# The first unit's attention transfers go through a paced queue, v loads follow the visit, and one pair of activations moves

## The chip, the cores and the metric

The kernel runs on one core of one Trainium2 chip. A core has a matrix engine (TensorE, PE in the profile, with its weight loads as PEld), a vector engine (VectorE, DVE), an activation engine (ScalarE, ACT), a general engine (GpSimd, POOL) and a fifth instruction queue without arithmetic (SyncE, SP), which in this kernel issues most DMA transfers. Each engine works through its own list of instructions in order and waits on semaphores for the others. The metric is the device time of one execution in microseconds, the median of several runs.

## The reference

Two computations follow each other. First comes attention with normalized q and k, over 8 batches, 12 heads, 448 positions and a head size of 64, in float32:

```python
def rmsnorm(x, g):
    rms = np.sqrt(np.mean(x * x, axis=-1, keepdims=True) + 1e-06)
    return x / rms * g
q_n, k_n = (rmsnorm(q, g_q), rmsnorm(k, g_k))
scores = scale * np.matmul(q_n, k_n.transpose(0, 1, 3, 2))
attn = np.exp(scores - np.max(scores, axis=-1, keepdims=True))
attn = attn / (np.sum(attn, axis=-1, keepdims=True) + 1e-09)
return np.matmul(attn, v)
```

Its result, laid out as 3584 tokens by 768 features, goes through a feed-forward layer with 2048 hidden features:

```python
h = np.maximum(x @ w_in, 0.0)
return (h * h @ w_out)
```

## The kernel before, in words

**Units and pairs.** Heads are taken two at a time, so that 64 + 64 features fill the 128 partitions: 48 pairs, six to a batch. The feed-forward layer takes two batches at a time; this is a *unit*, four in all. The matrix products of the feed-forward layer are done in Strassen-like forms (seven products in place of eight), in the later units two levels deep.

**What runs beside what.** The first twelve pairs have nothing beside them (`visit_alone`). From then on the attention of the next two batches is woven into the feed-forward layer of the two before. `ffn(u)` is a generator: each `yield` hands out one step of matrix products, with its cost. `run(until)` takes steps until a cost is reached; after each step it may convert a piece of weights, make sums of weights, and take the next pieces of attention work from the queues `tasks` and `pool_tasks`. Between two calls of `run` stands a *visit* of a pair, which puts down scores, exponentials and the product with v of the neighbouring pair. The *first unit* is the stretch in which `first` is true while `ffn(0)` runs, here some 137 to 530 us of the span: one level of Strassen (`first_products` at L909, `second_products` at L1077 and L1138), in four blocks of some 96 us.

**What the first unit does besides.** It also reads the weights. Each piece of 384 KB comes as 32-bit words into one of three buffers (`load_weights`, L1232 and L1237). ACT splits it (`split_words`, L1251 to L1253), DVE joins it (L1264, L1284, L1288), and the buffer is free for the piece after the next two. Then the sums that the products need are made (L1364), and the forms for the later units are stored in DRAM: five large stores for each block (`raw`, L1314 and L1316), ten sums made on DVE (L1324) in four buffers named `more`, each stored at L1342, and finished `out_sb` tiles at L1366.

**Attention's transfers.** For a pair of the later batches, q and k are loaded (`load_qk`, normalized on POOL at L217), q is stored to DRAM (`store_q`, name `q_rows`), and both are read back in 32-column blocks, two halves for each head (`load_blocks`), so that DVE can transpose them block by block (`turn_blocks`, L351). A load of q's blocks waits for the store. v comes with `load_v` (L361, and L368 for the last 64 positions), issued by SP in the first unit and by ACT later. Where ACT's Exp (L426) reads the scores and writes `wT`, the products at L503 and the sums of weights at L546 read that.

**Queues.** `transfer` issues a transfer on SP at once in the first unit; in the later units (`slowly`) it puts it into the queue `transfers`, from which `follow_transfers(most)` takes one or two after each step. Both appear in the profile at L315 or L319. SP's list is in the order in which all these calls are made. The code that decides:

```python
if slowly:
    transfers.append((to, some))
else:
    nc.sync.dma_start(to, some)
```

**Deep products.** In the later units `deep_products` runs step (k, n) in the order (k, 0), (k-1, 2), (k, 1), (k-1, 3). PSUM results are put away by DVE (L948, L958) or ACT (L952, L960), and a table `then` says after which step ACT applies ReLU and square to a finished quarter (`activate`, L1020 and L1021).

Of the kernel before, what the change touches and what calls it, by code (L numbers as in the profile page):

```python
# [223 lines left out]
def program(ctx, tc, rows, v, g, wide, ones, moe_w_in, moe_w_out, out, shift):  # L224

    nc = tc.nc
# [59 lines left out]
    def values_of(i):  # L286

        if i % 2:
            return [0, 1, 2] if joint(i) else [NJ, 0, 1, 2]
        return [0, 1, 2, NJ]  # L290
# [4 lines left out]
    def alone(i):  # L295

        return pairs[i][0] < 2
# [9 lines left out]
    def room_for_blocks(i, x):  # L307
        return rows.room(i)[:, x].rearrange("p g h d -> p (g h d)")[:, ds(i % 2 * S, S)]

    def transfer(to, some):  # L310

        if slowly:
            transfers.append((to, some))
        else:
            nc.sync.dma_start(to, some)  # L315

    def follow_transfers(most):
        for _ in range(min(len(transfers), most)):
            nc.sync.dma_start(*transfers.popleft())  # L319

    def store_q(i):

        if not i % 2:
            through[i // 2] = dram.tile([2, S, 2 * D], F32, name="q_rows", tag="q_rows", bufs=2)
        to = through[i // 2]
        transfer(
            to[i % 2, 0 : NJ * P].rearrange("(j p) c -> p j c", p=P),
            rows.part(i, 0)[:, 0:NJ].rearrange("p j h d -> p j (h d)"),
        )
        if not i % 2:  # L330
            for odd in range(2):
                transfer(
                    to[odd, NJ * P : S],
                    rows.room(i)[ds(odd * D, D), 0, NJ].rearrange("p h d -> p (h d)"),
                )

    def load_blocks(i, x):
        b, c = pairs[i]
        for e in range(2):
            source = through[i // 2][i % 2, :, ds(e * D, D)] if x == 0 else rows.qk[1][b, 2 * c + e]  # L340
            for half in range(2):
                transfer(
                    room_for_blocks(i, x)[ds(e * D + half * SIDE, SIDE)].rearrange(
                        "p (t n) -> p t n", n=SIDE
                    ),
                    source[:, ds(half * SIDE, SIDE)].rearrange("(t p) n -> p t n", p=SIDE),
                )

    def turn_blocks(i, x):
        dst = att.tile([P, S], F32, name="qT" if x == 0 else "kT")  # L350
        nc.vector.transpose(dst, room_for_blocks(i, x))  # L351
        if x == 0:
            nc.scalar.mul(dst, dst, g)  # L353
        turned[i, x] = dst

    def load_v(i):
        b, c = pairs[i]
        queue = nc.sync if first else nc.scalar
        values[i] = io.tile([P, NJ, 2, D], F32, name="vt", tag="vt")
        for e in range(2):  # L360
            queue.dma_start(  # L361
                values[i][:, :, e],
                rows.in_chunks(i, v[b, 2 * c + e, 0 : NJ * P]),
            )
        for odd in range(2):
            if joint(i) != (i % 2 == odd) or joint(i) and i % 2 == 0:
                h = 2 * (c - i % 2 + odd)
                queue.dma_start(  # L368
                    lasts[odd][ds(odd * D, D)],
                    v[b, h : h + 2, NJ * P : S].rearrange("h p d -> p h d"),  # L370
                )

    def rescale(i, x):
        rows.power(i, x)
        if x == 0 or shift:
            rows.scale(i, x, nc.gpsimd)

    def turn(i, x):

        tr = banks[7 - x if i < 2 or alone(i - 2) else 0]  # L380
        dst = att.tile([P, S], F32, name="qT" if x == 0 else "kT")
        for j in range(NJ):
            nc.tensor.transpose(
                tr[:, ts(j, P)], rows.part(i, x)[:, j].rearrange("p h d -> p (h d)"), ident
            )
        nc.tensor.transpose(
            tr[:, ts(NJ, P)], rows.room(i)[:, x, NJ].rearrange("p h d -> p (h d)"),
            wide[:, ds(i % 2 * LASTS, P)],
        )
        if x == 0:  # L390
            nc.vector.tensor_scalar(out=dst, in0=tr[:, 0:S], scalar1=g, scalar2=None, op0=ALU.mult)
        else:
            nc.scalar.copy(dst, tr[:, 0:S])
        turned[i, x] = dst
# [95 lines left out]
    def attend(i, some):  # L490

        order = values_of(i)
        for n in some:
            m = order[n]
            if joint(i) and m == NJ:
                attend_both(i)
                continue  # L500
            mine = ds(i % 2 * LASTS, LASTS) if m == NJ and shift else ds(0, P)
            for e in range(2):
                nc.tensor.matmul(  # L503
                    values_bank(i)[ds(e * D, D), :],
                    lhsT=lasts[i % 2][mine, e, :] if m == NJ else values[i][:, m, e, :],
                    rhs=weights[key_of(i, m), e][mine], start=n == 0, stop=n == len(order) - 1,
                )
# [426 lines left out]
    def deep_products(u, blk, hid, sums_, second):  # L934
# [83 lines left out]
        def activate(name, t):  # L1018
            dst = to[name][:, t]
            nc.scalar.activation(dst, dst, AF.Relu)  # L1020
            nc.scalar.activation(dst, dst, AF.Square)  # L1021

        then = {
            (3, 3): [lambda: activate("11", 0), lambda: activate("11", 1)],
            (4, 2): [lambda: join("12", 0, "22")], (4, 3): [lambda: join("12", 1, "22")],
            (5, 2): [lambda: join("22", 0)],
            (5, 3): [lambda: join("22", 1), lambda: activate("12", 0)],
# [392 lines left out]

    def run(until):
        nonlocal spent, slowly
        slowly = not first
        while spent < until:
            cost = next(stream)
            spent += cost
            if deep_to_make:
                deep_to_make.popleft()()
            make_sum()
            end_join()  # L1430
            while first and late and late[0] <= spent:
                late.popleft()
                convert()
            arrive()
            follow_plan(2 if first else 1)
            run_tasks(2 if cost > COST_OUT else 1)

    def run_tasks(most):
        for name, some in (("others", tasks), ("pool", pool_tasks)):
            for _ in range(0 if name in held else min(len(some), most)):  # L1440
                some.popleft()()
        follow_transfers(most)

    def run_all():
        before = set(held)
        held.clear()
        while tasks or pool_tasks:
            run_tasks(len(tasks) + len(pool_tasks))
        held.update(before)
        follow_transfers(len(transfers))  # L1450

    def drain():
        for _ in stream:
            pass
        while tasks or pool_tasks or transfers:
            run_all()
        arrive(True)
        while any(some is MARK for some in plan):
            before = len(plan)
            follow_plan(1)  # L1460
            assert len(plan) < before
# [8 lines left out]

    def load_qk(i):
        if i <= last:
            rows.load(i, SimpleNamespace(dma_start=transfer))

    def new_acc():
        return ffn_p.tile([P, DM], F32, name="acc", tag="acc", bufs=2 * NT + 1)

    def square(i, x, room, engine=None):
        if i <= last:
            rows.square(i, x, room[:, 0 : 4 * P], engine)  # L1480

    def normalize(i, x):
# [107 lines left out]
    def visit_whole(i):  # L1590
        nonlocal free_bank
        run_all()
        free_bank = 3 if i % 2 else 1
        if i <= last and not shift:
            for m in slots_of(i, 0):
                score(i, m)
        if shift:
            attend_all(i - 1)
        else:
            for n in range(len(values_of(i - 1))):  # L1600
                attend(i - 1, (n,))
                forget(i - 1, (n,))
                if i <= last and n < 2:
                    weigh(i, n)
            if i % 2 == 0:
                both_denominators(i - 2)
        if i <= last:
            weigh_slots(i, 1)
            load_v(i)
        if not shift:  # L1610
            if i % 2:
                nc.scalar.copy(rests[i], banks[0][:, 0:S])
                xts[pairs[i - 1]] = new_x()
                nc.scalar.copy(xts[pairs[i - 1]], values_bank(i - 1))
            else:
                tasks.append(lambda: invert_both(i - 2))
            if i <= last:
                additions(i)
        if shift or i % 2:
            prepare(i + 3)  # L1620
        else:
            tasks.append(lambda: tasks.append(lambda: prepare(i + 3)))
# [7 lines left out]
    with tc.manual_schedule(engines=ENGINES):  # L1630
# [8 lines left out]
        for i in range(len(pairs) + 1):  # L1639
            for n in range(1 if whole(i) else VISITS):  # L1640
# [16 lines left out]
                if x == unit:  # L1657
# [3 lines left out]
                        run(COST if first else LATER)  # L1661
                    elif first:
                        run(COST_IN + 1)
                slowly = not first and x < unit
                if whole(i):
                    visit_whole(i)
                else:
                    visit_among(i, n)
        run(LATER)
        drain()  # L1670
        for _ in ffn(B // 2 - 1):
            follow_plan(1)

# [28 lines left out]
```

## Time and profile before

| | |
|---|---|
| time, median of 3 runs | 1451.51 us (1450.36 to 1451.99) |
| the profiled execution | 1451.19 us, its span 1449.1 us |
| PE busy | 1394.8 us, 96% of the span |
| DVE, ACT, POOL busy | 796.5, 584.0, 800.9 us |
| 137 to 530 us (first unit) | PE busy 367.11 of 393.00 us, DMA busy share 0.66 |
| 530 to 1449.1 us | PE busy 904.10 of 919.10 us, DMA busy share 0.48 |

The profiled execution's time is its span and 2.1 us around it, and lies 0.3 us under the median. Idle time is read as the length of a stretch less the time in which PE is busy: 25.9 us in the first unit, 15.0 us in all that follows it. A busy PE is not one at its full clock: the page has a row with the granted clock, in tenths.

### The profile page before, as it was taken

The page shows a single profiled execution, that of the slowest core. Times are in us where ns is not written, and L with a number is a line of the kernel's source. Part 1 is how long each engine was busy: PE and PEld are TensorE (multiplying, and loading weights), DVE is VectorE, ACT ScalarE, POOL GpSimd, SP SyncE. Part 2 cuts the span into 40 slices and gives each one's busy share as a digit, 9 for nine tenths or more (in the row PEclk, how much of TensorE's full clock was granted, in tenths as well). Part 3 has the DMA queues.
Part 4 walks back from the last instruction along what each step waited for, and adds up shares of the span by engine and source line. Part 5 has one row for each costly group of instructions (what it writes and reads, how often), then busy time and mean ns, then how long its engine had stood idle before and what let it go on. Part 6 is the DMA issues. An engine that isn't in the chain of part 4 may idle for free.

```text
span 1449.1 us, 18279 instructions
## 1 busy us (share of the span) xinstructions
PE 1394.8 (96%) x5772; PEld 838.0 (58%) x5772; DVE 796.5 (55%) x1627; ACT 584.0 (40%) x1126; POOL 800.9 (55%) x802
## 2 busy tenths in 40 slices
PE   7989999889899899999999999999999999999998
PEld 3333444344344457485666747566674859688694
DVE  5996466787686764344445564334544554244443
ACT  6874466545545433443342423444242312221220
POOL 5667664564545687567485786846663664140412
PEclk9999999999899999999999999999999999999999
DMA  5555746766776886373655746455551726234132
GB/s 145 148 158 150 192 107 157 211 175 162 201 201 159 273 263 189 64 220 104 196 141 155 210 136 184 138 188 136 174 140 32 256 71 236 100 115 158 58 142 79
DMA packets 378926, 229.08 MB, mean 158 GB/s; under 512 B 271940, under 2 KB 347588, under 8 KB 374724
## 3 DMA queue, kind: packets, MB, share of 16 engines
q1 hardware_dynamic: 352160, 213.85, 50.7%
q10 hardware_dynamic: 26660, 13.97, 3.3%
q8 instruction: 48, 0.79, 0.2%
q14 instruction: 58, 0.48, 0.1%
HBM read 172.49 MB, written 55.25 MB: 157 GB/s over the span
## 4 chain that ended last, share of the span: by engine, by line
PE 79%; POOL 4%; ACT 4%; DMA 3%; SPq 3%; DVE 3%; issue 3%; ACTq 0%; DVEq 0%; POOLq 0%
PE bank L1138 28%; PE bank L963 20%; PE bank L418 9%; PE bank L503 8%; PE bank L909 5%; PE bank L1077 4%; SPq L315 1%; DMA words<-in_moe_w_out_dram 1%; PE bank L529 1%; POOL sum L445 1%; POOL sums L1063 1%; PE bank L546 1%; ACT hid L1021 1%; PE bank L515 1%; ACT wT L426 1%
## 5 line engine op out<-in xcount | busy, mean ns | idle before, releaser
L1191 DVE TENSOR_TENSOR acc<-acc,bank 128x384 f32<-128x384 f32 x324 | 174.0, 550 | 228.7 <-PE bank L1138 203.8
L963 PE MATMUL bank<-xT,in_sb 128*128 128x224 f32 x1344 | 288.6, 354 | 0.2
L1138 PE MATMUL bank<-out_sb,hid 128*128 128x384 f32 x768 | 272.0, 490 | 6.2 <-DVE acc L1191 3.4
L963 PEld LDWEIGHTS bank<-xT,in_sb 128*128 128x128 f32 x1344 | 252.7, 190 | 11.3 <-issue 4.3
L1138 PEld LDWEIGHTS bank<-out_sb,hid 128*128 128x128 f32 x768 | 143.5, 190 | 114.3 <-ACT hid L1021 10.0
L426 ACT ACTIVATE wT<-bank,rr 128x448 f32<-128x448 f32 x288 | 161.5, 630 | 118.2 <-PE bank L418 104.4
L1138 PE MATMUL bank<-out_sb,sums 128*128 128x384 f32 x576 | 205.4, 489 | 0.8 <-DVE acc L1191 0.8
L202 POOL TENSOR_TENSOR rr<-ms,minus_half 128x8 f32<-128x8 f32 (+1 forms) x96 | 147.3, 1535 | 85.7 <-DVE ms L195 72.4
L948 DVE TENSOR_TENSOR hid<-hid,bank 128x224 f32<-128x224 f32 x312 | 111.6, 384 | 126.5 <-PE bank L963 102.5
L418 PE MATMUL bank<-qT,kT 64*128 64x448 f32 (+1 forms) x768 | 169.6, 575 | 3.7 <-ACT qT L353 2.5
L1138 PEld LDWEIGHTS bank<-out_sb,sums 128*128 128x128 f32 x576 | 108.1, 190 | 84.0 <-issue 7.0
L909 PE MATMUL bank<-xT,in_sb 128*128 128x448 f32 x336 | 136.9, 562 | 0.2 <-DVE hid L1047 0.2
L418 PEld LDWEIGHTS bank<-qT,kT 64*128 64x128 f32 (+1 forms) x768 | 58.2, 174 | 106.3 <-issue 74.8
L1016 POOL TENSOR_TENSOR hid<-hid 128x448 f32<-128x448 f32 x24 | 27.2, 1141 | 163.9 <-DVE hid L948 148.1
L445 POOL TENSOR_TENSOR sum<-sum,wT 128x448 f32<-128x448 f32 (+1 forms) x96 | 111.4, 1183 | 8.7 <-ACT wT L426 8.1
L1020 ACT ACTIVATE hid<-hid 128x448 f32<-128x448 f32 x96 | 54.9, 572 | 134.9 <-POOL hid L1016 80.0
L909 PEld LDWEIGHTS bank<-xT,in_sb 128*128 128x128 f32 x336 | 64.4, 197 | 73.9 <-issue 64.1
L503 PE MATMUL bank<-wT,vt 128*64 128x448 f32 x480 | 102.8, 549 | 0.0
L1077 PE MATMUL bank<-out_sb,hid 128*128 128x384 f32 x256 | 89.2, 495 | 0.0
L963 PE MATMUL bank<-more,in_sb 128*128 128x224 f32 x288 | 75.2, 355 | 3.4 <-ACT part L960 1.9
L567 POOL COPY few<-few 32x14 f32<-32x14 f32 x48 | 9.0, 188 | 123.7 <-DVE few L565 121.7
L179 ACT ACTIVATE squares<-qk 128x512 f32<-128x512 f32 (+1 forms) x68 | 39.4, 579 | 85.0 <-DVE ms L192 43.3
(129 smaller groups left out, 1878.1 us busy)
## 6 DMA issues: line engine op xcount, KB each, us to landing
out_sb<-out_forms SPq DMA_DIRECT2D x24, 1536.0 KB, 7.2
in_sb<-in_deep SPq DMA_DIRECT2D x64, 384.0 KB, 4.5
in_sb<-in_deep SPq DMA_DIRECT2D x80, 256.0 KB, 4.0
words<-in_moe_w_in_dram SPq DMA_DIRECT2D x32, 384.0 KB, 3.6
words<-in_moe_w_out_dram SPq DMA_DIRECT2D x32, 384.0 KB, 3.3
out_forms<-out_sb SPq DMA_DIRECT2D x8, 1536.0 KB, 7.1
qk<-in_q_dram SPq DMA_DIRECT2D x96, 96.0 KB, 2.7
qk<-in_k_dram SPq DMA_DIRECT2D x96, 96.0 KB, 2.6
```

The source lines that it names most:

```text
L202: self.nc.gpsimd.tensor_tensor(out=self.rr[i][:, x, 0 : self.count(i)], in0=ms, in1=self.minus_half.to_broadcast(list(ms.shape)), op=ALU.pow,)
L418: nc.tensor.matmul(sc[some], lhsT=turned[p, 1][r, keys], rhs=turned[p, 0][r, :], start=True, stop=True,)
L426: nc.scalar.activation(new_weights((i, m), e), sc, AF.Exp, scale=rows.rr[i][:, 1, 2 * m + e : 2 * m + e + 1],)
L445: nc.gpsimd.tensor_tensor(out=sums[i, e][some], in0=left[some], in1=weights[key_of(i, m), e][some], op=ALU.add)
L503: nc.tensor.matmul(values_bank(i)[ds(e * D, D), :], lhsT=lasts[i % 2][mine, e, :] if m == NJ else values[i][:, m, e, :], rhs=weights[key_o ...
L909: nc.tensor.matmul(ps, lhsT=w_sb[:, IN.index(left), c, :], rhs=forms[u, c][right], start=first and c == 0, stop=c == NK - 1, skip_group_ch ...
L948: nc.vector.tensor_tensor(out=quarter(name, n), in0=quarter(base, n), in1=ps, op=ALU.add)
L963: nc.tensor.matmul(ps, lhsT=left, rhs=right, start=start, stop=stop, skip_group_check=True)
L1020: nc.scalar.activation(dst, dst, AF.Relu)
L1077: nc.tensor.matmul(ps, lhsT=hid[a].rearrange("p t e s -> p t (e s)")[:, t, ds(NT * P, P)], rhs=w_sb[t][:, 2 * a + half, :], start=(a, t) = ...
L1138: nc.tensor.matmul(ps, lhsT=lefts[left][:, t, ts(tt, P)], rhs=w_sb[t][:, OUT.index(right), :], start=first and t == 0, stop=t == 1, skip_g ...
L1191: nc.vector.tensor_tensor(out=acc, in0=acc, in1=ps, op=ALU.add)
```

## The change

Five things change.

1. In the first unit, too, transfers of attention go into the queue: `run` sets `slowly = True` for every unit, and visits do so unless they begin a unit. `run` takes two of them after each step of the first unit (`run_tasks(most, 2 if first else most)`); `run_all` no longer empties the queue in the first unit, and in the later ones empties it only if other tasks are left.
2. Each transfer carries a key, such as `("v", i)` or `("blocks", i, x)`. `ensure(key)` stands ahead of what reads the data (`turn_blocks`, `turn`, `rescale`, `square`, `attend`) and issues the queue up to that key if it has not been issued.
3. `load_v` goes through that queue in the first unit.
4. In `visit_whole` (the later units) `load_v` is put at the head of `tasks`, so that it is called after the next step, and not inside the visit.
5. In `deep_products`, `activate("11", 0)` moves from step (3, 3) to (4, 1), which is one step earlier in the order above, and `activate("11", 1)` to (5, 1).

```diff
-    def transfer(to, some):
-        if slowly:
-            transfers.append((to, some))
-        else:
-            nc.sync.dma_start(to, some)
+    def transfers_of(*key):
+        def transfer(to, some):
+            if slowly:
+                transfers.append((key, to, some))
+            else:
+                nc.sync.dma_start(to, some)
+        return SimpleNamespace(dma_start=transfer)

     def follow_transfers(most):
         for _ in range(min(len(transfers), most)):
-            nc.sync.dma_start(*transfers.popleft())
+            nc.sync.dma_start(*transfers.popleft()[1:])
+
+    def ensure(*key):
+        while any(some[0] == key for some in transfers):
+            follow_transfers(1)
...
     def turn_blocks(i, x):
+        ensure("blocks", i, x)
...
     def load_v(i):
-        queue = nc.sync if first else nc.scalar
+        queue = transfers_of("v", i) if first else nc.scalar
...
     def attend(i, some):
         order = values_of(i)
+        for n in (i, i + 1 if joint(i) and i % 2 == 0 else i):
+            ensure("v", n)
...
-            (3, 3): [lambda: activate("11", 0), lambda: activate("11", 1)],
+            (4, 1): [lambda: activate("11", 0)], (5, 1): [lambda: activate("11", 1)],
...
     def run(until):
-        slowly = not first
+        slowly = True
...
-            run_tasks(2 if cost > COST_OUT else 1)
+            most = 2 if cost > COST_OUT else 1
+            run_tasks(most, 2 if first else most)

-    def run_tasks(most):
+    def run_tasks(most, to_send=0):
...
-        follow_transfers(most)
+        follow_transfers(to_send)

     def run_all():
         while tasks or pool_tasks:
             run_tasks(len(tasks) + len(pool_tasks))
+            if not first:
+                follow_transfers(len(transfers))
-        follow_transfers(len(transfers))
...
         if i <= last:
             weigh_slots(i, 1)
-            load_v(i)
+            tasks.appendleft(lambda: load_v(i))
...
-                slowly = not first and x < unit
+                slowly = x < unit
```

The lists of instructions of the two programs, engine by engine, stand as follows. PE's list is the same. In the first unit the lists of DVE, ACT and POOL are the same too, and only SP's differs, from some 160 us on; it holds the same transfers in another order. In the later units DVE, ACT and POOL have the same instructions with some of them exchanged with neighbours.

More of the change, by code (lines that the diff above doesn't have):

```diff
@@ L324, in store_q @@
             through[i // 2] = dram.tile([2, S, 2 * D], F32, name="q_rows", tag="q_rows", bufs=2)
-        to = through[i // 2]
-        transfer(
+        to, queue = through[i // 2], transfers_of("q", i)
+        queue.dma_start(
             to[i % 2, 0 : NJ * P].rearrange("(j p) c -> p j c", p=P),
@@ L331, in store_q @@
             for odd in range(2):
-                transfer(
+                queue.dma_start(
                     to[odd, NJ * P : S],
@@ L341, in load_blocks @@
             for half in range(2):
-                transfer(
+                transfers_of("blocks", i, x).dma_start(
                     room_for_blocks(i, x)[ds(e * D + half * SIDE, SIDE)].rearrange(
@@ L373, in rescale @@
     def rescale(i, x):
+        ensure("qk", i)
         rows.power(i, x)
@@ L378, in turn @@
     def turn(i, x):
+        ensure("qk", i)
         tr = banks[7 - x if i < 2 or alone(i - 2) else 0]
@@ L1454, in drain @@
             pass
-        while tasks or pool_tasks or transfers:
+        while tasks or pool_tasks:
             run_all()
@@ L1472, in load_qk @@
         if i <= last:
-            rows.load(i, SimpleNamespace(dma_start=transfer))
+            rows.load(i, transfers_of("qk", i))
     def new_acc():
@@ L1479, in square @@
         if i <= last:
+            ensure("qk", i)
+            ensure("qk", i - i % 2)
             rows.square(i, x, room[:, 0 : 4 * P], engine)
@@ L1670, in program @@
         drain()
+        assert not transfers
         for _ in ffn(B // 2 - 1):
```

## The prediction

> **What bounds the kernel now.** I read the page first, then the stretches of 50 us, then PE's waits, then the timelines of PE, ACT and SP around the longest wait.
>
> The first part of the page and its row of the granted clock: PE is busy for 96% of the span, so the kernel is bound by PE, and only PE's idle time or its slow clock can be won.
>
> ```profile
> PE 1394.8 (96%) x5772; PEld 838.0 (58%) x5772; DVE 796.5 (55%) x1627; ACT 584.0 (40%) x1126; POOL 800.9 (55%) x802
> PEclk9999999999899999999999999999999999999999
> ```
>
> The stretches of 50 us (columns: PE, PEld, DVE, ACT, POOL busy, granted clock, DMA share, GB/s) show where it sits. One stretch in two of the first unit is full; its neighbour loses 6 to 10 us, has a lower clock, and has the busier DMA.
>
> ```profile
> 200.00:250.00 50.00, 50.00 (x172) 23.22 (x169) 32.49 (x62) 30.58 (x60) 24.89 (x20) 1.00 0.49 123
> 250.00:300.00 50.00, 40.14 (x116) 18.24 (x115) 36.44 (x55) 23.74 (x47) 26.85 (x23) 0.93 0.76 212
> 350.00:400.00 50.00, 42.80 (x125) 19.57 (x123) 36.75 (x58) 26.42 (x52) 26.61 (x22) 0.90 0.74 209
> 450.00:500.00 50.00, 43.70 (x130) 20.14 (x130) 38.83 (x59) 20.52 (x41) 28.90 (x25) 0.93 0.81 233
> ```
>
> PE's waits over the span name the largest one: the sums of weights (L546) wait for ACT's Exp, four times.
>
> ```profile
> PE bank L546 <- ACT wT L426: 18.1, 4, 5.9
> PE bank L1138 <- DVE acc L1191: 4.3, 4, 2.0
> ```
>
> The timelines of PE, then ACT, then SP around the longest of the four:
>
> ```profile
> 273.20 1.76 PE L546 MATMUL bank<-sum,ones 128*64 128x448 f32 x4 [5.92 <-ACT wT L426]
> 274.89 6.69 PE L909 MATMUL bank<-xT,in_sb 128*128 128x448 f32 x12
> ```
>
> ```profile
> 268.34 0.54 ACT L1251 ACTIVATE words<-words 128x384 f32<-128x384 f32 x1 [10.54 <-DMA words<-in_moe_w_out_dram]
> ```
>
> ```profile
> 248.81 4.34 SPq L1316 DMA_DIRECT2D in_deep<-in_sb  x2
> 253.25 2.55 SPq L315 DMA_DIRECT2D q_rows<-qk  x3
> 257.54 1.89 SPq L315 DMA_DIRECT2D qk<-q_rows  x4
> 259.48 2.40 SPq L315 DMA_DIRECT2D qk<-in_q_dram  x4
> 261.92 2.43 SPq L315 DMA_DIRECT2D qk<-in_k_dram  x4
> 264.46 0.53 SPq L1237 DMA_DIRECT2D words<-in_moe_w_out_dram  x1
> ```
>
> ACT stands for 10.54 us before a piece of weights, and the Exps that PE needs are behind it. The buffer of that piece was free at 255.38 (end of DVE's L1288), but SP issued the load only at 264.46: ahead of it stood three stores of q, a wait of 1.7 us for them to land, and twelve loads of about 0.5 us each. The same figure recurs at 373 and 475 us, with waits of 4.74 and 5.29 us, and in small at 177.55 (2.14 us).
>
> **What the Trainium skill says.** "Perfetto Trace Analysis", section "DMA Instruction — HWDGE (DVE, Sync)": the issuing sequencer first waits for its semaphores, then holds the descriptor generator, and only then is free for its next instruction. So one waiting transfer holds all behind it; the trace agrees (1.7 us above, and 22.1 us in 14 waits of L315 for q_rows between 100 and 540 us). "DMA: Bandwidth & Descriptors", section "Issuing engines are not separate DMA queues": all issuing engines share the same DMA engines, so an order in a queue saves issue time and waits, not bandwidth; here the DMA share is 0.66 over the first unit, so bandwidth isn't the limit on average. "TensorE: Matmul & The Clock Gate", section "What's actually happening": after an idle window of about 3.4 us the array runs at half clock until it has been busy for about as long. The trace agrees: the L909 group behind the stall takes 6.69 us where twelve such matmuls take 4.78 (at 262.50), and the four of L546 take 1.76 against 0.97 (at 440.27).
>
> **The change, part by part.**
>
> *Order on SP, first unit.* No transfer goes away; about 0.5 us each is paid as before. What moves is what stands ahead of the weight loads. In SP's new list the load of the first stall stands after the five large stores and two of the three stores of q; the read-back and the eight loads come after it. Worked for the three blocks, with end of ACT's Exps = the later of its two inputs (weights landed and split; DVE's L1047) and then L1048 and L1049 (1.05 us) and four Exps (2.2):
>
> Block 1: SP is free at 255.1 and the buffer at 255.4; issue 255.5, landing after 3.8 us as before, 259.3, three splits 1.5 us, 260.8. L1047 on DVE ends at 265.1, after 12.5 us of DVE work without a gap, so DVE is now the later. Exps end at 268.4; PE is ready at 267.28. The wait goes from 5.92 to 1.1: 4.8 us won.
> Block 2: buffer free 356.8, landing 4.3 later; L1047 ends 365.6, Exps 368.9, PE ready 368.7. From 4.74 to 0.2: 4.5.
> Block 3: buffer free 457.7; L1047 ends 467.4, Exps 470.7, PE ready 469.6. From 5.29 to 1.1: 4.2.
> The clock behind each: L546 0.8 and L909 1.9, 1.3 (6.05) and 1.8 (6.56) us, that is 2.7, 2.1 and 2.6. A wait near 1 us is not followed by a slow group (after the three waits at 292.8 to 299.2, of 2.00, 0.84 and 1.11 us, matmuls keep their speed), so I count all of it: 7.4.
> Block 0: at 161 us the third `in_deep<-more` store was behind k's, q's and the read-back's transfers until 168.74, and DVE waited for its buffer to 171.3; in the new list it follows two loads. 2.1 us won.
> Sum: 4.8 + 4.5 + 4.2 + 7.4 + 2.1 = 23.0 us won.
>
> *What becomes late instead.* The displaced loads now stand between the `more` stores, out_forms and weight loads. Two costs, neither shown by the trace of before. First, the buffers `more`: DVE has waited 33.7 us for these stores, and three of them with one or two loads of 0.5 us ahead of them now stand behind a 1.5 MB out_forms store that takes 7.2 us to land, as before. It moves DVE by up to 1 us in three places (around 287, 387 and 486 us), where DVE already made PE wait 3.95 us (292.8 to 299.2) and 2.46 us (387.17, L418 for qT). From -4 (these waits shrink, since all stands earlier) to +4; I take +2. Second, the block loads: from their last issue to DVE's transposition there were 23 to 98 instructions of all engines, and there are now 4 to 29 in a dozen groups (4 at 496.4, 12 at 299.1 and 418.0, 11 at 513.5). A read-back lands 2.4 us after its issue, a k block load after 2.8. SP runs ahead of the other lists (at 299.1 the loads were out 12 us ahead), so most still land in time. Behind the waiting transposition on DVE stand the L1191 additions that free PE's banks. Lower bound 0; upper one 2.8 us in each of ten groups, 28; I take +3, one late group in three with PE's banks covering part. `ensure` forces nothing in the first unit: at two per step the queue is always past the key.
>
> *v loads and activations.* In the first unit v is still issued some 10 us or more ahead of L503, and other products cover it; nothing, or up to its 3.6 us to landing if that lead were gone. In the later units the three or four issues on ACT (0.41 and 0.68 us at 535 us) no longer stand ahead of the copies of `rest`, `xT` and `hid`. PE's waits for L960 there are 2.0 us (`hid`, twice) and 1.9 (`part`, three times), with 1.26 more at 538.52. The moved activations take 1.15 of 2.3 us away from before `part`. Up to 5.2 us; the deferred issues delay L952 by the same 1.8 us once, so from +3 to -5; I take -2. POOL's sums and DVE's transpositions exchange places by a step; q's transposition stands at least ten matmuls of the program ahead of its use, so nothing.
>
> Sum: -23.0 + 2 + 3 - 2 = -20 us. On the profiled execution's 1451.19 this is 1431.2; the median is 0.3 above, so 1431.5.
>
> **The rivals.**
> *Half:* DVE becomes the bound. For: in all three stalls L1047 is only 1 us or so from binding, and a DVE lag carries into the second products; DVE is busy 73 to 78% in these stretches. Against: its gaps of 3.3 to 4.5 us for `more` behind L1047 go. If half of the 13.5 us and of the clock's 7.4 stays: about 1442.
> *All of it:* the waits at 292 to 299 and 387 go too (3.95, 2.46 and 1.6 us of slow clock behind it): about 1419.
> *Nothing:* the gains are eaten by equal waits elsewhere, or weights are late for another reason (their DMAs are behind the five large stores, 2.2 MB, in any order): 1451.
> *Slower:* late block loads. DVE stops at L351 in place of ACT at L1251, and PE's banks run out. There are some 27 groups in the first unit; the 23 us are gone when each costs PE over 0.85 us on average, or when eight of them cost 2.8. Stalls long enough for the slow clock come on top. At 1.3 us each: 35 - 23 = +12, 1463. Against: the lead of SP, and landing times under 3 us.
>
> **How the numbers follow.** Main case 0.64, 1424 to 1439; half 0.15; all 0.06; nothing 0.05; slower 0.10. The range from 1420 to 1448 holds the main case, half and most of "all": a little over 0.8. Under 0.2% (2.9 us, about what a measurement tells from no change) lies "nothing". Faster 0.85, same 0.05, slower 0.10.
>
> **What would show it.** PE's wait L546 for L426 under 5 us in total; ACT's longest wait for w_out words under 4 us in place of 10.5; no stretch of half clock after 130 us but the end; the words of each block issued within 1 us of their buffer's release; stretches 250:300, 350:400 and 450:500 at 45 us of PE or more. New waits of DVE's L351 for qk loads are the price; over 15 us of them, with PE waiting on L1191, would make the slower case. Wrong, too, if L1047 starts later against PE than now.

## The result: no change that can be told

The changed kernel takes 1451.5 us (median of 12 runs, 1448.48 to 1458.07) against 1450.49 us before (12 runs). The ratio is 1.0007, with a 95% interval from 0.9992 to 1.0022. I had predicted 1431.5 us.

The first part of the page after the change, with its row of the granted clock. PE's busy time has hardly moved (1394.8 before).

```profile
PE 1393.2 (96%) x5772; PEld 838.2 (58%) x5772; DVE 797.2 (55%) x1627; ACT 584.3 (40%) x1126; POOL 801.7 (55%) x802
PEclk9999999999899999999999999999999999999999
```

The stretches of 50 us, columns as in the prediction. The same stretches are short of PE as before: 42.46 us (40.14 before), 42.74 (42.80), 40.06 (43.70). The first lacks 2.3 us less, the second as much, the third 3.6 us more.

```profile
200.00:250.00 50.00, 50.00 (x164) 23.44 (x163) 34.48 (x66) 31.49 (x63) 24.94 (x20) 1.00 0.58 141
250.00:300.00 50.00, 42.46 (x130) 19.59 (x129) 37.81 (x59) 25.50 (x51) 27.87 (x23) 0.93 0.73 206
350.00:400.00 50.00, 42.74 (x135) 18.98 (x134) 37.20 (x58) 25.75 (x52) 28.92 (x23) 0.90 0.74 216
450.00:500.00 50.00, 40.06 (x125) 17.93 (x124) 35.60 (x56) 18.26 (x36) 30.54 (x27) 0.97 0.84 248
```

PE's waits have changed their names, though. (Lines have shifted: L546 of before is L559, L426 is L437, L1138 and L1191 are L1151 and L1204, L418 and L353 are L429 and L362, L351 is L360, L1047 is L1060, L1324 and L1342 are L1337 and L1355.) The wait for ACT's Exp was 18.1 us and is 3.0. In its place PE waits 12.9 us, not 4.3, for DVE's additions that free its banks, and 6.9 us for one transposed q.

```profile
PE bank L1151 <- DVE acc L1204: 12.9, 4, 5.6
PE bank L429 <- ACT qT L362: 6.9, 1, 6.9
...
PE bank L559 <- ACT wT L437: 3.0, 3, 1.3
```

PE's timelines, first around 273 us of before (now 264), then the two new places, and last the same two places in the kernel before:

```profile
264.05 0.97 PE L559 MATMUL bank<-sum,ones 128*64 128x448 f32 x4 [1.31 <-ACT wT L437]
264.96 4.78 PE L922 MATMUL bank<-xT,in_sb 128*128 128x448 f32 x12
```

```profile
285.49 2.92 PE L1151 MATMUL bank<-out_sb,hid 128*128 128x384 f32 x4 [5.63 <-DVE acc L1204]
288.21 4.45 PE L1151 MATMUL bank<-out_sb,sums 128*128 128x384 f32 x8
```

```profile
378.84 1.76 PE L429 MATMUL bank<-qT,kT 64*64 64x448 f32 x4 [6.85 <-ACT qT L362]
380.53 7.04 PE L1090 MATMUL bank<-out_sb,hid 128*128 128x384 f32 x16
```

```profile
292.83 1.56 PE L1138 MATMUL bank<-out_sb,hid 128*128 128x384 f32 x4 [2.00 <-DVE acc L1191]
387.17 0.98 PE L418 MATMUL bank<-qT,kT 64*64 64x448 f32 x4 [2.46 <-ACT qT L353]
```

The old stall is gone, with its slow clock: 1.31 us instead of 5.92, and twelve matmuls in 4.78 us instead of 6.69. But 20 us later PE stands for 5.63 us, and again works at a low clock behind it: four matmuls take 2.92 us, and 1.56 before. At 379 us it is the same: 6.85 us of wait, and four matmuls in 1.76 us instead of 0.98.

**Where the time went.** PE runs the same 5,772 matmuls in the same order, so I set them side by side, and read off how far PE is ahead of the kernel before (negative) at a given time of before, taken at the last matmul that begins by then. The last column belongs to an experiment further down.

| time of before, us | changed kernel | what lies in between | run e8 |
|---|---|---|---|
| 140 | -2.4 | | -1.4 |
| 260 | -4.5 | stall of block 0 gone | -4.0 |
| 280 | -11.8 | words stall of block 1 gone: -7.3 | -11.4 |
| 300 | -6.8 | PE waits for L1204: +5.0 | -12.5 |
| 380 | -13.3 | words stall of block 2 gone: -6.5 | -18.9 |
| 400 | -7.6 | PE waits for qT: +5.7 | -21.5 |
| 480 | -13.9 | words stall of block 3 gone: -6.3 | -26.7 |
| 520 | -4.2 | waits for L1204 in block 3: +9.7 | -23.4 |
| 560 | +0.7 | start of unit 1: +4.9 | -22.6 |
| 900 | -0.4 | | -23.6 |
| 1445 | +0.5 | | -23.2 |

What the change aimed at was won, 22.2 us in four places, and 25.3 us were lost in four others. The early difference up to 140 us is no part of it: SP's order is still the same there, and before had a window of half clock at 108 us that this execution of the changed kernel had not.

**What stopped PE at 285 us.** DVE's timeline ahead of it, of the changed kernel:

```profile
268.18 0.56 DVE L1337 TENSOR_TENSOR more<-more,in_sb 128x384 f32<-128x384 f32 x1 [2.27 <-DMA in_deep<-more]
...
274.51 0.56 DVE L1337 TENSOR_TENSOR more<-in_sb 128x384 f32<-128x384 f32 x1 [1.72 <-DMA in_deep<-more]
...
277.52 0.63 DVE L360 STREAM_TRANSPOSE qT<-qk 128x448 f32<-128x448 f32 x1
279.65 1.28 DVE L1337 TENSOR_TENSOR more<-in_sb 128x384 f32<-128x384 f32 x1 [1.49 <-DMA in_deep<-more]
...
284.89 1.01 DVE L1204 TENSOR_TENSOR acc<-acc,bank 128x384 f32<-128x384 f32 x2
```

DVE stops three times for one of the four buffers `more` (L1337), whose store to DRAM has not landed yet, and the additions L1204 stand behind. DVE reaches them at 284.89 us, 7.3 us sooner than before (292.23). PE stands ready for them at 279.86 us, 11.0 us sooner than before (290.83). The 3.6 us between the two come on top of the 2.00 us that it waited there before: 5.63 us.

### The profile page after: what moved, and what is told of

Read it like the earlier page. It is cut to its first block, busy times and chain, and to the rows that moved or that the text cites. A ratio compares the mean times of both kernels' runs of the same rounds, so it can differ in the third digit from the quotient of the medians.

```text
span 1449.9 us, 18283 instructions
## 1 busy us (share of the span) xinstructions
PE 1393.2 (96%) x5772; PEld 838.2 (58%) x5772; DVE 797.2 (55%) x1627; ACT 584.3 (40%) x1126; POOL 801.7 (55%) x802
## 4 chain that ended last, share of the span: by engine, by line
PE 77%; DMA 5%; POOL 5%; DVE 4%; ACT 3%; issue 3%; SPq 2%; ACTq 0%; DVEq 0%; POOLq 0%
PE bank L1151 27%; PE bank L976 19%; PE bank L429 9%; PE bank L516 8%; PE bank L922 6%; PE bank L1090 4%; DMA in_deep<-more 2%; POOL sums L1076 1%; DMA out_dram<-acc 1%; PE bank L542 1%; ACT hid L1033 1%; ACT hid L1034 1%; POOL hid L1029 1%; POOL sum L456 1%; PE bank L528 1%
## 5 line engine op out<-in xcount | busy, mean ns | idle before, releaser
L1204 DVE TENSOR_TENSOR acc<-acc,bank 128x384 f32<-128x384 f32 x324 | 173.8, 550 | 230.5 <-PE bank L1151 203.7
L1151 PE MATMUL bank<-out_sb,hid 128*128 128x384 f32 x768 | 273.8, 492 | 11.9 <-DVE acc L1204 9.0
L1151 PEld LDWEIGHTS bank<-out_sb,hid 128*128 128x128 f32 x768 | 144.2, 191 | 121.3 <-DVE acc L1204 11.5
L1151 PE MATMUL bank<-out_sb,sums 128*128 128x384 f32 x576 | 208.2, 495 | 3.9 <-DVE acc L1204 3.9
L437 ACT ACTIVATE wT<-bank,rr 128x448 f32<-128x448 f32 x288 | 161.7, 631 | 117.7 <-PE bank L429 100.2
L429 PE MATMUL bank<-qT,kT 64*128 64x448 f32 (+1 forms) x768 | 170.4, 575 | 8.1 <-ACT qT L362 6.9
L1151 PEld LDWEIGHTS bank<-out_sb,sums 128*128 128x128 f32 x576 | 109.5, 192 | 88.6 <-issue 6.8
L922 PE MATMUL bank<-xT,in_sb 128*128 128x448 f32 x336 | 131.9, 546 | 0.3 <-DVE hid L1060 0.3
L429 PEld LDWEIGHTS bank<-qT,kT 64*128 64x128 f32 (+1 forms) x768 | 58.5, 173 | 109.8 <-issue 70.2
L456 POOL TENSOR_TENSOR sum<-wT 128x448 f32<-128x448 f32 x48 | 57.5, 1209 | 76.2 <-PE bank L568 75.4
L362 ACT ACTIVATE qT<-qT,g 128x448 f32<-128x448 f32 x34 | 22.7, 667 | 125.8 <-DVE qT L360 125.8
```

Of the source, the lines that this page charges most:

```text
L429: nc.tensor.matmul(sc[some], lhsT=turned[p, 1][r, keys], rhs=turned[p, 0][r, :], start=True, stop=True,)
L437: nc.scalar.activation(new_weights((i, m), e), sc, AF.Exp, scale=rows.rr[i][:, 1, 2 * m + e : 2 * m + e + 1],)
L456: nc.gpsimd.tensor_tensor(out=sums[i, e][some], in0=left[some], in1=weights[key_of(i, m), e][some], op=ALU.add)
L922: nc.tensor.matmul(ps, lhsT=w_sb[:, IN.index(left), c, :], rhs=forms[u, c][right], start=first and c == 0, stop=c == NK - 1, skip_group_ch ...
L1151: nc.tensor.matmul(ps, lhsT=lefts[left][:, t, ts(tt, P)], rhs=w_sb[t][:, OUT.index(right), :], start=first and t == 0, stop=t == 1, skip_g ...
L1204: nc.vector.tensor_tensor(out=acc, in0=acc, in1=ps, op=ALU.add)
```

## The theories

*Theory A:* the words stall of before was a cover. While PE stood for late weights, DVE made up its own lag, which comes from its waits for `more`. Take the words stall away and DVE's lag stops PE in blocks 1 and 2; each of the two delays is worth next to nothing alone.

*Theory B:* the queue sends what it displaces too late (v, the k blocks of block 3, what is left at the start of unit 1), and that ate the gain.

In all ratios below, the kernel before on the same chip is 1.

## One part of the change at a time

The first run undoes parts four and five, the second makes them alone.

```diff
 e1, on the changed kernel
-            tasks.appendleft(lambda: load_v(i))
+            load_v(i)
...
-            (4, 1): [lambda: activate("11", 0)], (5, 1): [lambda: activate("11", 1)],
+            (3, 3): [lambda: activate("11", 0), lambda: activate("11", 1)],
```

> The changed kernel with its fourth and fifth parts undone: v loads go out inside the visit again, and the two early activations stay at the old step. What remains is the queue, two transfers per step, and the asking by name. Theory A (the fixed stall of the weight words was a cover over VectorE's own lag, which now stops PE in blocks 1 and 2): within 2 us of the changed kernel, about 1450, with the same PE waits for L1204 and L429 (about 5 and 7 us) near 285 and 379 us. Theory B (the displaced v loads and other late transfers ate the gain): 1445 to 1448, the waits at the start of unit 1 (2.25 us for hid, 1.8 us for wT) gone and the rest faster.

Measured: 1454.14 us, ratio 1.0039 (1.0025 to 1.0053). Neither theory had the queue alone slower than before. PE waits 5.6 us for L1204 at 287 us and 6.9 us for qT at 379 us, as A said. But the place at the start of unit 1 got worse, not better, against B. ACT's timeline of this run there:

```profile
529.36 0.51 ACTq L370 DMA_DIRECT2D vt<-in_v_dram  x1
534.40 0.68 ACTq L377 DMA_DIRECT2D lasts<-in_v_dram  x1
535.12 0.53 ACT L1629 COPY rest<-bank 128x448 f32<-128x448 f32 x1 [5.23 <-DMA vt<-in_v_dram]
535.55 0.54 ACT L1631 COPY xT<-bank 128x448 f32<-128x448 f32 x1
535.98 0.55 ACT L973 COPY hid<-bank 128x448 f32<-128x448 f32 x1
```

The issue of the `lasts` load (L377) waits on ACT's queue for some 4.5 us, and `rest`, `xT` and `hid` stand behind it; PE then waits 5.70 us. In the changed kernel the same load waits too, but behind these copies, and PE loses 2.25 us:

```profile
532.78 0.56 ACT L973 COPY hid<-bank 128x448 f32<-128x448 f32 x1
536.30 0.69 ACTq L377 DMA_DIRECT2D lasts<-in_v_dram  x1
537.03 0.35 ACT L965 COPY hid<-bank 128x224 f32<-128x224 f32 x1 [3.68 <-DMA out_dram<-acc]
```

So part four does not cost there, as theory B had it; it softens what the queue costs. What holds the `lasts` load can be read from the traces. Every transfer of these programs uses one of eight semaphores, taken in turn whatever queue issues it, and its issue waits until the transfer that had the same semaphore before has landed: in both traces this holds for all 916 issues on the six semaphores whose landings are recorded in full. The last to have the semaphore of `lasts` was a store of `out_dram`, which ACT had issued 10.8 us earlier in this run and 10.6 us earlier in the changed kernel; in both, a landing on that semaphore is recorded 0.02 us before `lasts` is issued.

> The kernel before with only the fourth and fifth parts: v loads one task later from unit 1 on, activations moved, no queue in the first unit. Theory A: 1450 to 1452, no measurable change. Theory B: 1452 to 1456, since the wait of the `lasts` load on ACT at the start of unit 1 shows here too.

Measured: 1447.96 us, ratio 0.9989 (0.9980 to 0.9998), a small gain. It has two places. At 530 to 550 us PE gains 1.2 us, and near 873 us 2.2 us: PE's waits for ACT's and DVE's `hid` and `part` there are 3.3 us before and 0.5 us in this run.

## The late k blocks

In block 3 SP issues nine loads of `in_deep` for the next unit, and the queue leaves the last two loads of k's blocks behind them. SP's and DVE's timelines of the changed kernel:

```profile
479.32 9.29 SPq L843 DMA_DIRECT2D in_sb<-in_deep  x9
488.66 1.18 SPq L322 DMA_DIRECT2D qk<-in_k_dram  x2
```

```profile
495.30 0.65 DVE L360 STREAM_TRANSPOSE kT<-qk 128x448 f32<-128x448 f32 x1 [8.70 <-DMA qk<-in_k_dram]
495.87 0.52 DVE L1204 TENSOR_TENSOR acc<-acc,bank 128x384 f32<-128x384 f32 x1
```

More than half of the 9.29 us is one wait, of the fourth of the nine loads, for a store of `out_dram` that ACT issued at 481.52 us and that had the same semaphore before:

```profile
SPq L843 <- DMA out_dram<-acc: 4.9, 1, 4.9
```

Before had such a wait too, of 4.8 us, but in front of a read-back of q; the k blocks were already out.

The experiment empties the queue ahead of the nine loads:

```diff
                 make_all_deep()
                 if blk == NBLK - 1:
+                    follow_transfers(len(transfers))
                     for n in range(4):
```

> The changed kernel, but every transfer still in the queue is sent just ahead of the in_deep loads of block 3, so that the k blocks are not behind nine of them. Both theories: the 8.7 us wait of VectorE for kT near 495 us falls below 2 us and PE's 3.9 us wait at 496 with it. Theory A: 1446 to 1449, this is one of three places. Theory B: 1442 to 1446, this and what follows from it is the most of the loss.

Measured: 1443.23 us, ratio 0.9961 (0.9948 to 0.9975). The changed kernel gains about 7 us (1.0007 to 0.9961) from this line; DVE's wait of 8.7 us is gone, and PE keeps 8.2 us of lead at 520 us where it kept 4.2. It also loses only 0.4 us at the start of unit 1, rather than 4.9, so most of that loss hangs on the late k blocks. The time lies in theory A's range. PE's waits near 286 and 378 us stay (5.64 and 6.86 us).

## DVE's waits for `more`

Four runs go at DVE. The first leaves its derived pieces out:

```diff
-            made[n] = ffn_p.tile([P, 4, P], F32, name="more", tag="more", bufs=4)[:, 0:size]
-            left, right = [x() for x in (left, right)]
-            nc.vector.tensor_tensor(out=made[n], in0=left, in1=right, op=op)
+            made[n] = (right if n in (4, 5) else left)()
```

> The changed kernel without VectorE's 40 derived weight pieces (L1337): the piece that each is made from is stored in its place, so the stores and loads are the same in number and size, the values of units 1 to 3 are not the reference's, and VectorE neither makes the pieces nor waits for a `more` buffer (about 13 us of work and waits per block). Theory A: the PE waits near 285 and 379 us go, 1437 to 1443. Theory B: the loss is in transfers, which stay: 1447 to 1451.

Measured: 1436.33 us, ratio 0.9909 (0.9895 to 0.9922), just inside theory A's range. PE's lead is 15.3 us at 400 us (7.6 in the changed kernel) and 23.8 us at 500 us; then the late k blocks and the start of unit 1 take 13 us of it back (all this in the profiled execution, which at 1440.4 us is the slowest of its five).

> The kernel before (no queue in the first unit), with VectorE's 40 derived weight pieces left out in the way of the fourth run: the source pieces are stored in their places, the later units' values are not the reference's. Theory A (the words stall of before hid VectorE's lag, so VectorE's work was free there): 1446 to 1451, with the 18 us of PE waits for wT still there. If VectorE's lag is what made those waits: 1438 or less, the waits for wT gone.

Measured: 1461.89 us, ratio 1.0082 (1.0069 to 1.0095). This run does not tell what it was made for, since its edit brings a wait of its own: the stores now read `in_sb` itself, and DVE waits up to 16.3 us for them before it can fill that buffer again (28.3 us in two waits of L1264). Runs e4 and e6 have that wait too (17.6 us in e6), so their times are no lower bound.

> The changed kernel with both: no derived pieces and the k blocks ahead of the in_deep loads (values of the later units not the reference's). Theory A plus the late k blocks: the two add, 1426 to 1432, PE's gain on the kernel before 15 us or more at 500 us and kept to the end. If a stall taken away only moves on to the next: 1434 to 1437, as the fourth run alone.

Measured: 1431.52 us, ratio 0.9880 (0.9861 to 0.9899). The two gains add: within the range given for that.

The next two keep all the work. A derived piece is stored when two made pieces wait, so one step later than need be, and its buffer comes free that much later. The seventh run stores it a step sooner; the eighth sends it from ACT's queue.

```diff
 e7, with the line of e3
-            if len(to_keep) > 1 or not make:
+            if to_keep:
 e8, with the line of e3
-                nc.sync.dma_start(*to_keep.popleft())
+                nc.scalar.dma_start(*to_keep.popleft())
```

> The changed kernel with the k blocks ahead of the in_deep loads, and each derived piece stored one step sooner (one made piece waits instead of two), so that its buffer comes free a step of about 3 us sooner. Theory A: VectorE's waits for `more` in the first unit fall from 25 to under 12 us, PE's waits near 285 and 379 us shrink by 2 to 3 us each, 1436 to 1441. Against it: SyncE waits for the piece just made and holds up what is behind it, 1444 to 1449.

> As the seventh, but instead of sooner, the 40 stores of derived pieces go out from ACT's queue rather than SyncE's. Theory A: they leave as soon as made and take 40 issues of 0.5 us off SyncE; VectorE's waits for `more` fall below 12 us, 1435 to 1441. Against it: ACT's sequencer waits for VectorE, the exponentials behind it come later, PE waits for wT; 1445 to 1455.

Measured: e7 1430.16 us, ratio 0.9870 (0.9854 to 0.9886); e8 1426.58 us, ratio 0.9841 (0.9828 to 0.9854). Both beat what I expected of them, and both beat either kernel of this case. DVE's waits for `more` in the first unit fall from 25.5 us in e3 to 6.4 and 0.9 us. In e7 all stores stay on SP, so the gain is not merely that SP has 40 issues fewer. In e8 (its lines stand one further on), PE's waits and the stretches of 50 us read:

```profile
PE bank L1152 <- DVE acc L1205: 7.5, 7, 1.8
...
PE bank L559 <- ACT wT L437: 3.0, 3, 1.3
```

```profile
250.00:300.00 50.00, 45.82 (x149) 21.05 (x148) 45.52 (x71) 27.60 (x54) 29.28 (x25) 1.00 0.82 238
350.00:400.00 50.00, 47.23 (x159) 21.59 (x158) 42.83 (x75) 28.69 (x56) 31.35 (x27) 1.00 0.82 237
450.00:500.00 50.00, 45.46 (x154) 21.44 (x155) 37.90 (x71) 15.16 (x29) 37.48 (x36) 1.00 0.87 268
```

The clock is full in all three, and PE has at least 45 us in each: this is the picture that I had predicted for the changed kernel. DVE in the first of them is busy for 45.52 of 50 us, from 37.81; it lost its waits, not its work. The span is 23.1 us shorter than that of before: PE is idle 14.4 us less (39.9, from 54.3), and its busy time is 8.7 us shorter (1386.1, from 1394.8). Matmuls in the half-clock windows of before take 10.4 us less, 1.4 of them at 108 us, ahead of anything that the edits touch; elsewhere 1.7 us are added.

## Each cause alone, and both

The last test puts the same edit of the stores on the kernel before, and on the changed kernel with the k blocks left late.

> The kernel before with one edit alone, the 40 stores of derived pieces from ACT's queue. Theory A (the late weight words bound the first unit of before, and VectorE's waits for `more` lay under them): 1446 to 1452, PE's 18 us of waits for wT still there. Rival (SyncE's queue is only too full, and 40 issues fewer free the words too): 1435 to 1442, the waits for wT under 8 us.

> The changed kernel with the stores on ACT's queue and the k blocks left behind the in_deep loads. If the two losses are separate and add: the eighth run plus the 6 to 8 us that the third run gained, 1432 to 1435. If the late blocks cost only where VectorE is already late: 1427 to 1430.

| | stores on SP | stores on ACT |
|---|---|---|
| kernel before | 1 | 0.9981 (0.9972 to 0.9989), 1447.68 us |
| changed kernel | 1.0007 (0.9992 to 1.0022), 1451.5 us | 0.9882 (0.9867 to 0.9896), 1433.13 us |
| changed kernel, k blocks early (e3, e8) | 0.9961 (0.9948 to 0.9975), 1443.23 us | 0.9841 (0.9828 to 0.9854), 1426.58 us |

On the kernel before, DVE's waits for `more` fall from 33.7 to 6.6 us, and 2.7 us of time come of it:

```profile
DVE more L1324 <- DMA in_deep<-more: 6.6, 5, 3.9
```

```profile
PE bank L546 <- ACT wT L426: 16.2, 3, 5.8
```

PE's waits for the words in blocks 1 to 3 are there as before (16.2 us; before, 16.0 of the 18.1). The 2.7 us were won in block 0, whose wait of 2.14 us is gone: there DVE's wait for a `more` buffer had made the Exps late, and the changed kernel wins the same 2.1 us. So in blocks 1 to 3 the stores alone give nothing.

If the two edits were independent, their ratios would multiply, to 0.9988 in the second row and 0.9942 in the third. Measured are 0.9882 and 0.9841. A further 1.0 to 1.1%, some 15 us, comes only of the two together: each delay covered the other. This is theory A, shown from both sides. That the changed kernel alone gains nothing at all is also due to its late k blocks; without them it gains 0.4%. They cost about 6 us with the stores on ACT and about 7 with the stores on SP. That cost is separate and adds, and theory B held for that one place.

## Two details on the fastest version

> The eighth run's kernel with parts four and five undone, as the first run did to the changed kernel, where that cost 4 us at the start of unit 1. If the later v load is worth something in itself: 1428 to 1432. If it only answered ACT's wait behind late out_dram stores at that place: no difference, 1425.5 to 1427.5.

Measured: 1430.86 us, ratio 0.9862 (0.9847 to 0.9876). Parts four and five are worth about 3 us also where the start of unit 1 no longer suffers, though the intervals overlap a little, and 2.6 us of the 3.9 us between the profiled executions is a window of half clock at 285 us, behind a stall of 1.52 us that e8 has too, without a window. The rest of it lies where e2 gained, near 873 us of before, and at 520 to 540 us.

> The eighth run's kernel with four transfers per step instead of two. If the pace matters (a batch of four ahead of a words load of the next step): the waits for wT rise from 3.0 us towards 6, 1428 to 1433. If two or four are one: 1425 to 1428.

Measured: 1430.63 us, ratio 0.9863 (0.9847 to 0.9879). The time is that of the first case, but not its reason: the waits for wT stay at 3.0 us, and PE has a new wait of 2.8 us for qT in block 2. That four per step are no better than two is shown; what makes the difference isn't.

## Why the prediction was wrong

*The stall and its size: right.* I predicted 4.8, 4.5 and 4.2 us of waits and 2.7, 2.1 and 2.6 us of slow clock in blocks 1 to 3, and 2.1 us in block 0: 23.0 us. The side-by-side gives 7.3, 6.5, 6.3 and 2.1: 22.2 us. What is left of the three waits is 1.31, 0.36 and 1.31 us, where I worked out 1.1, 0.2 and 1.1. ACT's 10.54 us for a piece of w_out have become 4.2 us at most.

*The `more` buffers, "I take +2": this is the step that failed.* I costed only what the new order of stores would change in DVE's waits, between -4 and +4 us. They did not grow; they fell from 33.7 to 25.1 us. What changed is that nothing covered them any more. My working ended at the next meeting of PE with its supplier, L546, and there I even found DVE within about 1 us of binding. I did not go on to the meetings after that, L1191 and L418, where PE's waits of before showed DVE last already: 2.00 us in the first of three waits, and 2.46 us. Carried on, the sum is short. At L1191 PE is ready 11.0 us sooner. DVE is 7.3 us sooner: 4.5 of them were there before block 1's stall, and in block 1 its waits for `more` shrink only from 8.6 to 5.9 us. So 2.00 us become 5.63, with a slow clock behind them. For qT in block 2 PE is ready 12.7 us sooner and qT 8.3, and 2.46 us become 6.85. Blocks 1 and 2 cost 5.0 + 5.7 = 10.7 us in place of 2.

*The block loads, "I take +3": mis-sized, and in another place.* One late group was enough. I had expected many groups late by a little, at most 2.8 us each, because SP runs ahead; I did not look at what SP itself waits for. The nine `in_deep` loads hold SP for 9.29 us, 4.9 of them in the wait for a store, and the two loads behind them came 8.70 us late. With e3's line PE is 4.0 us further ahead at 520 us and loses 0.4 us instead of 4.9 behind that; the whole is worth about 7 us by the times, inside my bounds of 0 to 28. The loss that stays in block 3 with e3 has two parts. One is DVE's lag, gone in e8. The other, 3.3 us at 510 us of before, e8 has as well:

```profile
DVE words L676 <- DMA xT<-x_rows: 3.6, 1, 3.6
```

That load is issued behind the nine `in_deep` loads too. It looks like one more late load, but no run moves it ahead, so that its place is the cause is not shown.

*The start of unit 1: not in the sum.* I costed part four there from -5 to +3 and took -2 with part five. On the kernel before, the two parts measured 1.6 us (e2), close to what I took. On the changed kernel they gained about 4.6 us (1.0039 to 1.0007), mostly by softening a wait on ACT's queue that the queue of part one brings; with that wait, the changed kernel still loses 4.9 us between 520 and 560 us, and 4.5 of these go with the late k blocks.

*The rivals.* "Nothing: the gains are eaten by equal waits elsewhere" is what happened, at a chance of 0.05; its mechanism is that of "half", DVE as the bound, which I had stopped at half the gain. The fault is in treating "DVE binds" and "late block loads" as cases that exclude each other, each with its own small price. They add: 10.7, 9.7 and 4.9 us are lost in turn, the first from DVE's lag, the second from that and the late k blocks, the third for the most part behind these.

*The signs.* L546's wait under 5 us: right. ACT's longest wait for w_out under 4 us: just missed, at 4.2. Words issued within 1 us of their buffer's release: 0.6, 1.2 and 0.3 us in blocks 1 to 3. DVE's waits for qk loads rose from 4.8 to 17.0 us, less than the 15 us more that I had named for the slower case. No half clock after 130 us, and 45 us of PE in three stretches: both failed, and pointed at once to the places. The last sign, L1047 later against PE than now, came true: its two at 281.69 of before start 10.0 us sooner while PE is 11.8 us ahead.

## What to carry to other kernels

When a stall is to be taken away, move the whole of PE's list forward by its length, and go through every later meeting with another engine, not only the next; an engine that was last there keeps PE waiting as long as before, and longer by whatever part of the gain it does not share (2.00 us became 5.63, and 2.46 became 6.85). A wait of a lagging engine is not priced by how the change alters it, but by what stops covering it. Two delays that cover each other both measure as worth little alone, so the one that seems free has to be tried together with the other; here moving one kind of store to another queue turned no change into 1.2%, and with one line more into 1.6%.

## What the runs showed of the hardware

The windows of half clock have a sharp edge. Over the 14 profiled executions, from 100 us to shortly before the end, each window began during a stall of PE or within 2 us of its end, and lasted 3.41 us or two or three times that. All of 30 stalls of 3.3 us or more had one, 16 of 21 between 2.2 and 3.3 us, and 4 of 94 between 0.8 and 2.2 us. So half clock is not a matter of stalls of 3.4 us and more alone, as the prediction took it, though below 2.2 us it is rare. One stall cut from 5.9 to 1.3 us gains more than its length, and one only shortened to 4 us need not: in block 1, e4 still had a stall of 4.70 us and a window of 3.4 us, and e8 had 1.52 and 1.23 us and none.
